# Reading the unsplit W_out blocks in one run: natural column order in a fused attention and MoE kernel

## The chip, the cores and the metric

The kernel runs on one core of one Trainium2 chip. The metric is the device time of one execution in microseconds. Three runs of the kernel before gave 651.16, 652.11 and 652.94 us; their median, 652.11 us, is the time before. The traced execution took 651.43 us, of which 649.9 us lie between its first and its last instruction.

## The reference

Attention with 4 sink tokens and a window of 128 over q, k, v of shape (4, 8, 768, 64), then a two-layer feed-forward block on the 3072 tokens that come out:

```
scores = (q @ k^T) / sqrt(64), masked to sinks and window
a      = exp(scores - max);  a = a / (sum + 1e-9)
x      = (a @ v)  as 3072 x 512
h      = x @ w_in                              (512 x 2048)
g      = max(h, 0) + alpha * min(h, 0)
out    = g @ w_out                             (2048 x 512)
```

The weights arrive as 64-bit floats and are turned into 32-bit ones on the chip.

## The kernel before

The tokens are cut into 12 chunks of 256 (`NCHUNK`), the hidden width of 2048 into 16 blocks of 128 (`NF`). For each chunk c the attention of 8 heads gives `xh` and `xl`, the two halves of x. For each block f, `gemm1(c, f)` multiplies x with block f of w_in into a PSUM bank, ScalarE and VectorE make g from it (L995, L996), and `gemm2(c, f)` adds g times block f of w_out (128 x 512) to the two output banks of the chunk, one for each half j of the tokens.

Most products are split: each factor is written as a high part of the type fp32r plus the rest, and three fp32r products (high x high, high x low, low x high) stand for the 32-bit one. In `gemm2` these are L1048, L1049 and L1046, three matmuls of 512 columns for each j. The split costs a cast on ScalarE and a subtraction on VectorE for g (L1001, L1002) and for the weights. In the first two chunks the first 8 blocks (`WHOLE = 8`, `c < 2 and f < WHOLE`) skip it: g and W_out stay whole, and `whole()` (L1035 to L1037) runs one native fp32 matmul for each j. A native fp32 matmul stands in the trace as two matmul instructions, so 2 chunks x 8 blocks x 2 halves give 64 of them at L1037.

The whole block lives in `entire` (128 x 512, written by `out_whole`, L449 to L452). When chunk 2 begins, `divide(f)` (L471 to L480) splits it: a cast to fp32r (L476, on ScalarE or VectorE) and a subtraction on VectorE (L479), 8 of each. From then on the block is read like the others, by `row` (L401, L402).

The order of columns: the host swaps the 512 columns of each W_out block (L1403) so that all even columns stand ahead of all odd ones. A matmul reads them through `rearrange("p (y x) -> p x y", y=2)`, which steps to and fro between the two halves of the row, 256 elements (1 KB) apart, and so meets the columns in their natural order. This alternating order is used for the split blocks and, before the change, for the whole ones at L1037 as well. `gemm1` reads x in the same way.

The order of instructions on each engine is written out by a planner. `Plan.draw` is a list scheduler: each operation has an engine and a cost in microseconds that the author gave it (for `whole()`, `2 * native(DM)`, which is 1.707), and at each step it takes the operation that can start first, with ties by rank. Each engine then runs its instructions in the planned order and waits on semaphores for what isn't ready. During chunks 0 and 1 the weights are loaded and converted as well: for each f < 8 ScalarE's L423 and VectorE's L427, L428, L440 (twice) and L453; for the other blocks L432, L435, L456, L462 and L465. The attention of chunk 1 is computed early in chunk 0's blocks, that of chunk 2 late in chunk 1's (`LATE = 11`).

Of the kernel before, what the change touches and what calls it, by code (L numbers as in the profile page):

```python
# [9 lines left out]
F32 = mybir.dt.float32  # L10
# [7 lines left out]
ALU = mybir.AluOpType  # L18

P = 128  # L20
B, H, S, D = 4, 8, 768, 64
DM, DF = 512, 2048
# [6 lines left out]
NF = DF // P  # L29
# [28 lines left out]
WHOLE = 8  # L58
# [28 lines left out]
class Plan:  # L87
# [20 lines left out]
    def held(self, tile_):  # L108
        v = Value(None)
        v.at = tile_  # L110
        return v
# [197 lines left out]
def dve(n, fast=False):  # L309
    return 0.07 + (0.52e-3 if fast else 1.04e-3) * n  # L310


def cast(n, psum=False):
    return (0.045 if psum else 0.092) + 0.84e-3 * n
# [22 lines left out]
def woven(n):  # L337
    return 0.003 + 0.4167e-3 * n


def native(n):
    return 1.667e-3 * n
# [3 lines left out]
ISSUE = 0.45  # L346
SINKLAG = 0.0
R_TAIL, N_TAIL, T_TAIL = 0.2, 0.65, 0.36


def program(ctx, tc, qk, pairs, vp, vq, vs, w, par, out):
    nc = tc.nc
# [5 lines left out]
    op, val, held = plan.op, plan.value, plan.held  # L358
# [36 lines left out]
    raws, fins = {}, {}  # L395
# [7 lines left out]


    def home(f):
        return f + NF - WHOLE if f < WHOLE else f

    def load_weights(f, engine="ACT"):
        raw = raws[f] = held(None)

        def run():
            raw.at = const.tile([P, 2 * DM, 2], I32, tag=f"w{home(f)}", name="wraw")
            (nc.sync if engine == "SP" else nc.scalar).dma_start(
                raw.at.rearrange("p (i x) w -> p i (x w)", i=2), w[f].bitcast(I32).rearrange("i p x -> p i x"))
        return op(engine, ISSUE if engine == "SP" else 0.12, run, writes=[raw] + (lent.get(home(f), []) if f < WHOLE else [raws[f - NF + WHOLE]]), nbytes=8 * P * 2 * DM)

    def convert_weights(f):
        raw, fin, wa = raws[f], Block(None), val("wa")
# [51 lines left out]

    def divide(f):  # L471
        fin, entire = fins[f], entires[f]

        def high(engine):
            fin.at[1] = const.tile([P, 2, DM], F32R, tag=f"out{f - 1}", name="wout")
            (nc.scalar.copy if engine == "ACT" else nc.vector.tensor_copy)(fin.at[1][:, 0], entire.at)  # L476
        op("ACT", cast(DM), lambda: high("ACT"), reads=[entire], writes=[(fin, 2)] + ([entires[f - 1]] if f else []),
           other=("DVE", dve(DM, True), lambda: high("DVE")))
        op("DVE", dve(DM), lambda: nc.vector.tensor_tensor(  # L479
            fin.at[1][:, 1], entire.at, fin.at[1][:, 0].bitcast(F32), ALU.subtract), reads=[entire, (fin, 2)], writes=[(fin, 3)])  # L480

    stage, vtile, vst = {}, {}, {}

    lent = {}
# [64 lines left out]
    part, alt = param[:, :4], param[:, 4:].bitcast(F32)  # L549
# [313 lines left out]
    turned = {}  # L863
# [143 lines left out]
    def gemm2(c, f, dst):  # L1007
        gh, gl = gs.pop((c, f))
        fin = fins[f]
        begin, end = (WHOLE % NF, (WHOLE - 1) % NF) if c == 2 else (0, NF - 1)  # L1010
        if f == begin:
            acc[c] = [val("pa"), val("s")] if c == 1 else [val("o"), val("o")]
        o2 = acc[c]
        if c == NCHUNK - 1 and f >= NF - 2:
            latest.append((f, fin, gh, gl))
            for j in range(2 if f == NF - 1 else 0):
                for x, fin, gh, gl in latest:
                    def last(j=j, x=x, fin=fin, gh=gh, gl=gl):
                        js = slice(j * P, (j + 1) * P)
                        nc.tensor.matmul(o2[j].at, gh.at[:, js], fin.row(0), start=False, stop=False)  # L1020
                        nc.tensor.matmul(o2[j].at, gh.at[:, js], fin.row(1), start=False, stop=False)
                        nc.tensor.matmul(o2[j].at, gl.at[:, js], fin.row(0), start=False, stop=x == NF - 1)
                    op("PE", 3 * woven(DM), last, reads=[fin, gh, gl], writes=[o2[j]], tail=R_TAIL)
                ob = val("ob")
                for n, cols in enumerate((slice(0, DM // 2), slice(DM // 2, DM)) if j else (slice(0, DM),)):
                    op("ACT", cast(cols.stop - cols.start, True), lambda ob=ob, j=j, cols=cols: nc.scalar.copy(ob.at[:, cols], o2[j].at[:, cols]),  # L1026
                       reads=[o2[j]], writes=[(ob, n)])
                    by, cost, engine = ("ACT", 0.1, nc.scalar) if n == j else ("SP", ISSUE, nc.sync)
                    op(by, cost, lambda ob=ob, j=j, cols=cols, engine=engine: engine.dma_start(dst(j)[:, :, cols], ob.at[:, cols]),
                       reads=[(ob, n)], nbytes=4 * P * (cols.stop - cols.start))  # L1030
            return
        if c < 2 and f < WHOLE:
            entire = entires[f]

            def whole():  # L1035
                for j in range(2):
                    nc.tensor.matmul(o2[j].at, gh.at[:, j * P:(j + 1) * P], entire.at.rearrange("p (y x) -> p x y", y=2),  # L1037
                                     start=f == begin, stop=False)
            op("PE", 2 * native(DM), whole, reads=[entire, gh], writes=o2, tail=N_TAIL)
            return  # L1040
        for lowpart in range(2):
            def some(lowpart=lowpart):
                for j in range(2):
                    js = slice(j * P, (j + 1) * P)
                    if lowpart:
                        nc.tensor.matmul(o2[j].at, gl.at[:, js], fin.row(0), start=False, stop=(f == end))  # L1046
                    else:
                        nc.tensor.matmul(o2[j].at, gh.at[:, js], fin.row(0), start=(f == begin), stop=False)  # L1048
                        nc.tensor.matmul(o2[j].at, gh.at[:, js], fin.row(1), start=False, stop=False)  # L1049
            op("PE", (2 if lowpart else 4) * woven(DM), some, reads=[fin, gl if lowpart else gh], writes=o2, tail=R_TAIL)  # L1050
        if f == end:
            for j in range(2):
                ob = val("ob")
                op("ACT", cast(DM, True), lambda ob=ob, j=j: nc.scalar.copy(ob.at, o2[j].at), reads=[o2[j]], writes=[ob],
           other=("DVE", dve(DM), lambda ob=ob, j=j: nc.vector.tensor_copy(ob.at, o2[j].at)) if 0 < c < 3 else None)
                op("SP", ISSUE, lambda ob=ob, j=j: nc.sync.dma_start(dst(j), ob.at), reads=[ob], nbytes=4 * P * DM)
            del acc[c]
# [109 lines left out]
    def dst(c):  # L1167
        return lambda j: out[c * QC:(c + 1) * QC].rearrange("(y j x) d -> j x y d", y=2, j=2)[j]
# [9 lines left out]
    n = 0  # L1178
# [35 lines left out]
    for a in pend:  # L1214
        gemm2(*a, dst(a[0]))
# [27 lines left out]
    gen = ctx.enter_context(tc.tile_pool(name="general", bufs=1))  # L1243
# [3 lines left out]
    wts = [fins[f].at for f in range(NF)]  # L1247
    with tc.If(bad != 0, label="general"):
        for f in range(NF):
            for i in range(2):  # L1250
                general_weights(nc, gen, w[f, i], wts[f][i])
        with tc.For_i(0, B, 1) as b:
            for cc in range(CPB):
                x = general(nc, gen, ptile, cc, b, qk5, vp5, nsink, window, ident)
                acc = [ptile("o", 2) for _ in range(2)]
                for f in range(NF):
                    general_moe(nc, gen, ptile, f, x, wts[f], alt, acc)
                for j in range(2):
                    ob = gen.tile([P, DM], F32, tag="ob", name="ob", bufs=3)
                    nc.scalar.copy(ob, acc[j])  # L1260
                    nc.gpsimd.dma_start(out5[b, cc, j], ob)
# [24 lines left out]
        nc.tensor.matmul(acc[j], gl[:, js], rows[0], start=False, stop=(f == NF - 1))  # L1286


def general_weights(nc, gen, src, dst):
    raw = gen.tile([P, DM, 2], I32, tag="wraw", name="wraw", bufs=2)  # L1290
    nc.gpsimd.dma_start(raw.rearrange("p x w -> p (x w)"), src.bitcast(I32))
    a = gen.tile([P, DM], I32, tag="wa", name="wa", bufs=2)
    low, high, af = raw[:, :, 0], raw[:, :, 1], a.bitcast(F32)
    nc.scalar.activation(af, high.bitcast(F32), AF.Abs)
    nc.vector.tensor_scalar(af, af, EXP_LOW, EXP_HIGH, op0=ALU.max, op1=ALU.min)
    nc.vector.tensor_scalar(a, a, 3, 0x3FFFFFFF, op0=ALU.logical_shift_left, op1=ALU.bitwise_and)
    nc.vector.scalar_tensor_tensor(a, high, -0x40000000, a, op0=ALU.bitwise_and, op1=ALU.bitwise_or)
    nc.scalar.activation(low, low.bitcast(U32), AF.Copy, scale=2.0 ** -29)
    nc.vector.tensor_tensor(a, a, low, ALU.add)
    nc.scalar.copy(dst[:, 0], af)  # L1300
    nc.vector.tensor_tensor(dst[:, 1], af, dst[:, 0].bitcast(F32), ALU.subtract)


def general(nc, gen, ptile, cc, b, qk5, vp5, nsink, window, ident):
# [118 lines left out]
```

## Time and profile before

| what | value |
|---|---|
| median of three runs | 652.11 us (651.16 to 652.94) |
| traced execution | 651.43 us, span 649.9 us |
| TensorE (PE) busy | 640.4 us, 99% of the span |
| VectorE (DVE) busy | 522.6 us, 80% |
| ScalarE (ACT) busy | 392.4 us, 60% |
| L1037, the native fp32 matmuls | 64, from 34.7 to 109.7 us, 36.5 us of busy time |

"Busy" for PE counts a modelled end of each matmul, and matmuls overlap: the duration of a matmul in the trace (705 ns at L1037) is not what it adds. What it adds is the distance from its start to the start of the next one. A first matmul after a slower one can show its start early, while it still queues behind it; the start after that one is then the reliable mark. PEld is the load of the stationary operand, which runs beside the matmul ahead of it.

### The profile page before, as it was taken

How to read it: one execution, taken by the hardware profiler on the slowest of the kernel's cores; microseconds unless marked ns; L12 is line 12 of the kernel's file. 1: busy time of each engine (PE TensorE's matmuls, PEld its weight loads, DVE VectorE, ACT ScalarE, POOL GpSimd, SP SyncE). 2: the span in 40 equal slices, each digit the busy share in tenths (PEclk: the TensorE clock that was granted, in tenths of full speed). 3: DMA queues.
4: the chain of work that ended last, by engine and by line, in shares of the span. 5: the costliest groups of instructions: out<-in, count | busy, mean ns of one | idle time of the engine just before them, and what ended most of it. 6: DMA issues, size and time to landing. Idle time of an engine off the chain costs nothing. (4 is left out here: it accounts for less than half of the span.)

```text
span 649.9 us, 13096 instructions
## 1 busy us (share of the span) xinstructions
PE 640.4 (99%) x4495; PEld 563.0 (87%) x4497; DVE 522.6 (80%) x1748; ACT 392.4 (60%) x1060; POOL 34.1 (5%) x115
## 2 busy tenths in 40 slices
PE   8999999989999999999999999999999999999997
PEld 3666667979998999999999999998999998998996
DVE  6998888997987987895996997895996997895332
ACT  6997677856646646645645754844754854752332
POOL 2120000000100000000100000000100000000000
PEclk9999999999999999999999999999999999999999
DMA  8776631333443444341633534432534424421001
GB/s 314 250 274 219 215 101 53 96 99 106 129 135 120 136 138 135 112 131 50 188 120 91 168 98 138 136 112 82 169 113 115 148 97 147 148 65 51 33 3 35
DMA packets 58825, 82.29 MB, mean 127 GB/s; under 512 B 9088, under 2 KB 35328, under 8 KB 58752
## 3 DMA queue, kind: packets, MB, share of 16 engines
q1 hardware_dynamic: 55200, 68.41, 33.3%
q10 hardware_dynamic: 3552, 12.98, 5.7%
q8 instruction: 37, 0.61, 0.4%
q14 instruction: 36, 0.29, 0.1%
HBM read 64.33 MB, written 17.04 MB: 125 GB/s over the span
## 5 line engine op out<-in xcount | busy, mean ns | idle before, releaser
L995 ACT ACTIVATE g<-bank,param 128x256 f32<-128x256 f32 x192 | 90.9, 473 | 94.4 <-PE bank L991 93.8
L991 PE MATMUL bank<-xh,win 128*128 128x256 f32 x768 | 140.5, 279 | 0.0
L991 PE MATMUL bank<-xh,w 128*128 128x256 f32 x768 | 139.1, 276 | 0.4 <-DVE g L996 0.4
L991 PEld LDWEIGHTS bank<-xh,w 128*128 128x128 f32 x768 | 120.9, 192 | 2.7 <-DVE g L996 1.0
L991 PEld LDWEIGHTS bank<-xh,win 128*128 128x128 f32 x768 | 120.8, 192 | 2.3 <-issue 1.6
L1001 ACT CAST gh<-g 128x256 fp32r<-128x256 f32 x176 | 70.6, 405 | 63.0 <-DVE g L996 62.4
L996 DVE TENSOR_TENSOR g<-bank,g 128x256 f32<-128x256 f32 x192 | 80.1, 420 | 33.8 <-ACT g L995 32.4
L991 PE MATMUL bank<-xl,win 128*128 128x256 f32 x384 | 105.7, 275 | 0.0
L991 PE MATMUL bank<-xl,w 128*128 128x256 f32 x384 | 105.6, 275 | 0.0
L700 ACT ACTIVATE pt<-pt,nm 128x260 f32<-128x260 f32 (+1 forms) x192 | 93.5, 489 | 16.5 <-DVE nm L694 16.2
L694 DVE CUSTOM_DVE_ANT_0 pt<-bank,masks 128x260 f32<-128x260 f32 (+1 forms) x192 | 71.2, 401 | 33.0 <-PE bank L680 29.3
L1002 DVE TENSOR_TENSOR gl<-g,gh 128x256 fp32r<-128x256 f32 x176 | 73.4, 421 | 17.6 <-ACT gh L1001 14.5
L991 PEld LDWEIGHTS bank<-xl,win 128*128 128x128 f32 x384 | 73.6, 192 | 2.3 <-issue 1.4
L991 PEld LDWEIGHTS bank<-xl,w 128*128 128x128 f32 x384 | 73.5, 192 | 1.2 <-issue 0.4
L1048 PE MATMUL bank<-w,gh 128*128 128x512 f32 x188 | 71.6, 381 | 0.0
L1049 PE MATMUL bank<-w,gh 128*128 128x512 f32 x188 | 71.2, 379 | 0.0
L641 ACT CAST kq<-stage 128x392 fp32r<-128x392 f32 (+1 forms) x80 | 39.1, 488 | 36.8 <-PE bank L680 28.2
L1048 PE MATMUL bank<-wout,gh 128*128 128x512 f32 x160 | 60.7, 379 | 0.0
L1049 PE MATMUL bank<-wout,gh 128*128 128x512 f32 x160 | 60.6, 379 | 0.0
L1046 PE MATMUL bank<-w,gl 128*128 128x512 f32 x188 | 56.4, 382 | 0.0
L1046 PE MATMUL bank<-wout,gl 128*128 128x512 f32 x160 | 47.7, 380 | 0.0
L745 POOL TENSOR_TENSOR sink<-pt,ri 128x8 f32<-128x8 f32 x80 | 20.2, 254 | 502.0 <-DVE ri L730 421.9
(150 smaller groups left out, 1106.3 us busy)
## 6 DMA issues: line engine op xcount, KB each, us to landing
stage<-qk SPq DMA_DIRECT2D x56, 324.0 KB, 2.9
wraw<-w ACTq DMA_DIRECT2D x12, 1024.0 KB, 5.2
swap<-comb SPq DMA_DIRECT2D x36, 256.0 KB, 2.0
comb<-swap SPq DMA_DIRECT2D x36, 256.0 KB, 3.0
stage<-qk SPq DMA_DIRECT2D x24, 260.0 KB, 2.7
out_dram<-ob SPq DMA_DIRECT2D x22, 256.0 KB, 2.7
v<-vq SPq DMA_DIRECT2D x24, 192.0 KB, 3.2
wraw<-w SPq DMA_DIRECT2D x4, 1024.0 KB, 9.2
```

The lines of the kernel that those rows point to most:

```text
L641: op("ACT", cast(KC - n), lambda: nc.scalar.copy(ks()[:, n:], k_raw()), reads=[st], writes=[(kq, "k")])
L694: o = op("DVE", dve(n), lambda: nc.vector.tensor_tensor_reduce(out=pt.at[:, u, w0], in0=s.at[:, w0], in1=masks[:, i, w0], scale=-0.125, sc ...
L700: op("ACT", exp(n), lambda: nc.scalar.activation(pt.at[:, u, w0], pt.at[:, u, w0], AF.Exp, bias=nm.at[:, h, u:u + 1], scale=-1.0, accum_ou ...
L745: op("POOL", 0.2, lambda: nc.gpsimd.tensor_tensor(sk.at[:, :, h], pt.at[:, :, P:P + NS], ri.at[:, :2].unsqueeze(2).broadcast_to([P, 2, NS] ...
L991: nc.tensor.matmul(h(), fin.win(part, ks), row, start=(kt == 0 and n == 0), stop=(kt == KT - 1 and n == 2))
L995: op("ACT", act(QC, True), lambda: nc.scalar.activation(g.at, h(), AF.Copy, scale=alt[:, f:f + 1]), reads=[bk, known("param")], writes=[g])
L996: op("DVE", dve(QC), lambda: nc.vector.tensor_tensor(g.at, h(), g.at, ALU.max), reads=[bk], writes=[g])
L1001: op("ACT", cast(QC), lambda: nc.scalar.copy(gh.at, g.at), reads=[g], writes=[gh])
L1002: op("DVE", dve(QC), lambda: nc.vector.tensor_tensor(gl.at, g.at, gh.at.bitcast(F32), ALU.subtract), reads=[g, gh], writes=[gl])
L1046: nc.tensor.matmul(o2[j].at, gl.at[:, js], fin.row(0), start=False, stop=(f == end))
L1048: nc.tensor.matmul(o2[j].at, gh.at[:, js], fin.row(0), start=(f == begin), stop=False)
L1049: nc.tensor.matmul(o2[j].at, gh.at[:, js], fin.row(1), start=False, stop=False)
```

## The change

The host leaves the columns of the first 8 W_out blocks in natural order and swaps only those of the other 8. `whole()` then reads `entire` in one run of 512 neighbouring elements. `divide` puts the columns into the alternating order: its cast and its subtraction read every second element of `entire` (steps of 8 bytes), twice 256, and write two runs of 256. The planned cost of `whole()` grows by 0.1 us, from 1.707 to 1.807. In `home` and `load_weights` an expression changes its form: with `NF = 16` and `WHOLE = 8`, `NF - WHOLE` and `NF // 2` are both 8, so every block gets the tile and the writes that it had. `general_weights` belongs to a branch that these inputs don't take.

```
     def home(f):
-        return f + NF - WHOLE if f < WHOLE else f
+        return f + NF // 2 if f < WHOLE else f
 ...
     def divide(f):
         fin, entire = fins[f], entires[f]
+        turned_ = lambda: entire.at.rearrange("p (x y) -> p y x", y=2)
+        part = lambda n: fin.at[1][:, n].rearrange("p (y x) -> p y x", y=2)
 ...
-            (nc.scalar.copy if engine == "ACT" else nc.vector.tensor_copy)(fin.at[1][:, 0], entire.at)
+            (nc.scalar.copy if engine == "ACT" else nc.vector.tensor_copy)(part(0), turned_())
 ...
-            fin.at[1][:, 1], entire.at, fin.at[1][:, 0].bitcast(F32), ALU.subtract), reads=[entire, (fin, 2)], writes=[(fin, 3)])
+            part(1), turned_(), part(0).bitcast(F32), ALU.subtract), reads=[entire, (fin, 2)], writes=[(fin, 3)])
 ...
             def whole():
                 for j in range(2):
-                    nc.tensor.matmul(o2[j].at, gh.at[:, j * P:(j + 1) * P], entire.at.rearrange("p (y x) -> p x y", y=2),
+                    nc.tensor.matmul(o2[j].at, gh.at[:, j * P:(j + 1) * P], entire.at,
                                      start=f == begin, stop=False)
-            op("PE", 2 * native(DM), whole, reads=[entire, gh], writes=o2, tail=N_TAIL)
+            op("PE", 2 * native(DM) + 0.1, whole, reads=[entire, gh], writes=o2, tail=N_TAIL)
 ...
-    w[:, 1] = inputs['moe_w_out'].reshape(NF, P, DM // 2, 2).swapaxes(2, 3).reshape(NF, P, DM)
+    w[:, 1] = inputs['moe_w_out'].reshape(NF, P, DM)
+    w[WHOLE:, 1] = inputs['moe_w_out'].reshape(NF, P, DM // 2, 2)[WHOLE:].swapaxes(2, 3).reshape(NF - WHOLE, P, DM)
```

## Rows read from the trace of the kernel before

**Rows 1.** Stages of the span: busy time (count) of each engine, clock, DMA.
```profile
34.60:51.00 16.40, 16.40 (x101) 10.16 (x100) 15.49 (x42) 14.57 (x37) 3.61 (x5) 1.00 0.67 228
51.00:66.00 15.00, 15.00 (x95) 10.21 (x94) 13.19 (x20) 11.06 (x21) 0.00 (x0) 1.00 0.64 227
66.00:98.00 32.00, 32.00 (x155) 20.46 (x154) 28.02 (x37) 23.76 (x36) 0.00 (x0) 1.00 0.49 167
98.00:110.40 12.40, 12.40 (x72) 9.27 (x71) 10.54 (x19) 9.99 (x17) 0.00 (x0) 1.00 0.13 51
110.40:150.00 39.60, 37.09 (x271) 33.03 (x271) 37.45 (x137) 25.95 (x73) 1.98 (x8) 1.00 0.28 85
250.00:600.00 350.00, 350.00 (x2578) 325.68 (x2576) 290.93 (x1050) 202.18 (x582) 16.33 (x57) 1.00 0.39 121
```

**Rows 2.** Line L1037: its matmuls, duration min/median/max in ns, first and last start.
```profile
L1037 PE MATMUL bank<-wout,g x64: 700/705/802, 34.7 to 109.7; 128*128 128x512 f32 x64
```

**Rows 3.** PE's instructions in order of time around 67 us: start, us, what.
```profile
67.01 0.28 PE L991 MATMUL bank<-xh,win 128*128 128x256 f32 x1
67.12 4.49 PE L1037 MATMUL bank<-wout,g 128*128 128x512 f32 x8
70.94 0.79 PE L991 MATMUL bank<-xh,win 128*128 128x256 f32 x1
71.56 0.28 PE L991 MATMUL bank<-xl,win 128*128 128x256 f32 x1
```

**Rows 4.** PE in order of time: fp32 operands read in one run.
```profile
33.74 0.71 PE L670 MATMUL bank<-stage 64*128 64x260 f32 x4
34.38 0.33 PE L719 MATMUL bank<-ident,pt 128*128 128x128 f32 x1
...
38.81 1.96 PE L873 MATMUL bank<-comb,v 128*64 128x256 f32 x24
40.70 0.71 PE L670 MATMUL bank<-stage 64*128 64x260 f32 x4
...
46.16 0.27 PE L719 MATMUL bank<-ident,pt 128*128 128x128 f32 x1
...
46.71 0.27 PE L720 MATMUL bank<-ident,pt 128*128 128x128 f32 x1
```

**Rows 5.** PE in order of time: fp32r, in one run (L680) and alternating (L1048).
```profile
113.18 0.29 PE L679 MATMUL bank<-kq 128*128 128x260 f32 x1
113.30 0.28 PE L680 MATMUL bank<-kq 128*128 128x260 f32 x1
113.43 0.38 PE L1048 MATMUL bank<-w,gh 128*128 128x512 f32 x1
113.64 0.38 PE L1049 MATMUL bank<-w,gh 128*128 128x512 f32 x1
```

**Rows 6.** L1037 alone in the first of these stages: PE busy (count), PEld busy (count).
```profile
34.60:51.00 16.40, 6.94 (x12) 1.99 (x12) 1.00 0.67 228
```

**Rows 7.** Groups by line and shape: count, busy us, mean ns, idle before.
```profile
L479 DVE TENSOR_TENSOR wout<-wout 128x512 fp32r<-128x512 f32 x8 | 5.5, 685 | 0.1
L476 ACT CAST wout<-wout 128x512 fp32r<-128x512 f32 x6 | 3.7, 620 | 3.1 <-DVE wout L479 3.1
L476 DVE CAST wout<-wout 128x512 fp32r<-128x512 f32 x2 | 0.8, 420 | 0.0
L440 DVE SCALAR_TENSOR_TENSOR wout<-wraw,wa 128x512 int32<-128x512 int32 x8 | 5.5, 691 | 0.0
```

**Rows 8.** Waits from 34.6 to 110.4 us: us, times, longest.
```profile
ACT g L995 <- PE bank L991: 10.6, 10, 2.4
```

**Rows 9.** Waits of PE from 110.4 to 150 us.
```profile
PE bank L815 <- DVE jk L741: 1.6, 2, 1.4
PE bank L991 <- DVE g L996: 0.4, 1, 0.4
```

More of the change, by code (lines that the diff above doesn't have):

```diff
@@ L414, in run @@
                 raw.at.rearrange("p (i x) w -> p i (x w)", i=2), w[f].bitcast(I32).rearrange("i p x -> p i x"))
-        return op(engine, ISSUE if engine == "SP" else 0.12, run, writes=[raw] + (lent.get(home(f), []) if f < WHOLE else [raws[f - NF + WHOLE]]), nbytes=8 * P * 2 * DM)
+        return op(engine, ISSUE if engine == "SP" else 0.12, run, writes=[raw] + ([raws[f - NF // 2]] if NF // 2 <= f < NF // 2 + WHOLE else lent.get(home(f), [])), nbytes=8 * P * 2 * DM)
     def convert_weights(f):
@@ L1250, in program @@
             for i in range(2):
-                general_weights(nc, gen, w[f, i], wts[f][i])
+                general_weights(nc, gen, w[f, i], wts[f][i], f < WHOLE and i == 1)
         with tc.For_i(0, B, 1) as b:
@@ L1286, in general_moe, with general_weights @@
         nc.tensor.matmul(acc[j], gl[:, js], rows[0], start=False, stop=(f == NF - 1))
-def general_weights(nc, gen, src, dst):
+def general_weights(nc, gen, src, dst, turned):
     raw = gen.tile([P, DM, 2], I32, tag="wraw", name="wraw", bufs=2)
@@ L1299, in general_weights @@
     nc.vector.tensor_tensor(a, a, low, ALU.add)
-    nc.scalar.copy(dst[:, 0], af)
-    nc.vector.tensor_tensor(dst[:, 1], af, dst[:, 0].bitcast(F32), ALU.subtract)
+    high, low = [dst[:, n].rearrange("p (y x) -> p y x", y=2) for n in range(2)]
+    af = af.rearrange("p (x y) -> p y x" if turned else "p (y x) -> p y x", y=2)
+    nc.scalar.copy(high, af)
+    nc.vector.tensor_tensor(low, af, high.bitcast(F32), ALU.subtract)
 def general(nc, gen, ptile, cc, b, qk5, vp5, nsink, window, ident):
```

## The prediction

> **What bounds the kernel now.** I read the stages first [rows 1]. From 250 us on, PE is busy all the time at a granted clock of 1.00 and VectorE (DVE) 290.93 of 350 us (83%): PE sets the pace, and the rest of the run begins as early as PE reaches it. Up to 110.4 us PE shows no idle time either. But other engines are close behind: DVE is busy 15.49 of 16.4 us (94.5%) from 34.6 to 51, with ScalarE at 14.57; then 51.75 of 59.4 us (87%) from 51 to 110.4; then 37.45 of 39.6 us (94.6%) from 110.4 to 150, and there PE does idle, 2.5 us. The reader is to see three stretches: PE and DVE nearly level, then PE ahead as the bound, then DVE as the bound.
>
> The next view is the line that changes. L1037 has 64 matmuls, from 34.7 to 109.7 us [rows 2]: all of them lie in the first two stretches. Its duration of 705 ns is a modelled one, so I take the spacing instead. Between the first matmul of a group of eight, at 67.12, and the first reliable start behind it, 71.56, lie the eight and one L991, which adds 0.11 (67.01 to 67.12): (4.44 - 0.11) / 8 = 0.541 us for each [rows 3]. All 64 are 34.6 us of PE.
>
> The last views are waits. From 34.6 to 110.4 us ScalarE's L995, the first step from `gemm1` to g, stands 10.6 us in 10 waits for PE [rows 8]: faster matmuls would be picked up. From 110.4 to 150 it is the other way round: PE waits 1.6 us for DVE's L741 and 0.4 for its L996 [rows 9]. L741 is chunk 2's softmax, which DVE must finish before the steady part begins.
>
> **The change, part by part.**
>
> *The moving operand of L1037 in one run.* Nothing is added or removed; each of 64 matmuls reads neighbours instead of stepping 1 KB to and fro. No row shows a native fp32 matmul of full width (128 columns of weights) with such a read, so I bound it. Six fp32 transposes of 128 columns, read in one run, begin 0.55 us apart from first to last, 0.11 each [rows 4]: for 512 columns, 0.44. The fp32 values of L873, two halves of the array's columns side by side, run 4 turns of 256 and 8 of 128 columns, 2048 in all, between 38.81 and 40.70, entry and exit included: 0.92 ns a column, 0.47 for 512 [rows 4]. The dear end is L670, fp32 in one run on two halves of the array's rows: two turns of 260 columns in 0.64 us, so 0.63 for 512 [rows 4]. Below the transposes I put the rate of one fp32r matmul twice, 2 x 0.215 = 0.43 [rows 5]. I take 0.44, from the transposes: like L1037 they use the whole array, with nothing beside them. So 64 x (0.541 - 0.44) = 6.5 us less PE time; the other values give 7.1 (0.43), 4.5 (0.47) and -5.7 (0.63, slower).
>
> The trace also holds a warning: for fp32r the alternating read is the cheaper one. L679 and L680 read 260 columns in one run and take 0.12 us each; L1048 reads 512 alternating in 0.21 [rows 5]. Scaled to 512 that is 0.24 against 0.21, 10% more for the single run. If fp32 followed fp32r, L1037 would go to 0.59 and the kernel lose 3.5 us. The Trainium skill speaks for the change here: "SBUF — State Buffer", under "Door 1: The DMA port swizzle", says that SBUF has lines of 16 bytes and that an access which moves to another line pays. By it every alternating read would be dear, and a run of four elements per line cheap. The fp32r rows don't agree with that, so I take the sum from the fp32 rows and not from the rule.
>
> *What of 6.5 us reaches the end.* In the first stretch are 12 of the 64 [rows 6], 1.2 us of the saving. DVE is busy 94.5% there, as in the stretch where it is the bound (94.6%) [rows 1]. So I count nothing for these 12. The other 52, 5.25 us, lie between 51 and 110.4 us, where DVE has 51.75 us of work in 59.4. If DVE can again be filled to 94.6%, it needs 54.7 us, so the stretch shrinks by 4.7 us at most. What DVE doesn't follow, PE loses later: the stretch after 110.4 is DVE's, and its PE waits grow by the same amount. With DVE filled to 92% it would be 3.2 us; with no idle left, all of the 5.25 and part of the 1.2. I take 4.7. What is late next is DVE's chain through chunk 2's softmax (L694, L741) up to about 150 us. Behind 150 us PE runs back to back, and nothing takes the gain back.
>
> *The split in `divide`.* Eight L479 on DVE (685 ns), six L476 on ScalarE (620) and two on DVE (420) now read every second element [rows 7]. Reads of that step cost DVE nothing in a two-input operation: L440 takes 691 ns for 512 elements of 8-byte step, against 685 for L479 [rows 7]. The two DVE casts run at twice that speed, and no row shows such a cast with a step; if they fell to L479's time it would be 2 x 0.27 = 0.5 us of DVE in the stretch where it counts. I take nothing, from L440's row, and keep 0.5 for the range. On ScalarE even 10% would be 0.4 us in all, beside its idle time (23.76 busy of 32 us [rows 1]); without that cover it would be those 0.4 us. The Trainium skill, "VectorE: DVE Perf Modes" under "Mode 2×_2P", asks of a one-source copy at double speed that both sides lie in SBUF and that the outermost dimension be even, not that the step be one; the pattern here is 2 x 256. By it the two casts stay at 420 ns; no row here shows it.
>
> *The planned cost.* The plan took 1.707 us for a pair of whole products; the trace has 4 x 0.541 = 2.16. Now it takes 1.807, against 4 x 0.44 = 1.76. A list scheduler may order differently from the first such pair on, on every engine, SP's and ScalarE's DMA issues too. No row gives that a price. I bound it by the waits that an order can make or spare in the DVE-bound stretch, some 2 us [rows 9], to either side, and take 0, because nothing in the rows points to one side.
>
> *The other edits* give the same tiles and writes (8 = 8), or lie in the branch not taken: 0.
>
> The sum: 651.43 - 4.7 = 646.7 us for the traced execution. It lies 0.7 us below the median of the runs, so I forecast 652.1 - 4.7 = 647.4.
>
> **The rivals.**
>
> *All of it arrives, or more.* DVE's idle time before 110 us follows from PE's lateness (10.6 us of ScalarE's waits [rows 8]), and an order planned at nearly the true cost may lose some of the 2 us of waits. For it: those waits; against it: DVE at 94.6% has not been filled further anywhere. 6.5 + 2 = 8.5 at most: 643.6 to 646, middle 645.3.
>
> *DVE takes it.* The conversions don't close up, and chunk 2's softmax starts almost where it did. For it: 94.6% and PE's wait for L741 [rows 1, 9]; against it: 7.65 us of DVE idle time between 51 and 110.4. A gain of 0.5 to 3 us: 649.1 to 651.6, middle 650.1.
>
> *The order of reading doesn't matter for native fp32.* Then L1037 stays at 0.541, the change doesn't do what it says, and 652.1 remains. For it: L670 reads in one run and needs 0.63 for 512, and fp32r gains nothing from it; against it: transposes and L873 [rows 4].
>
> *The single run is dearer.* PE, L1037, 64 times: at 0.59, as fp32r would have it, +3.5 us; at 0.63, as in L670, +5.7. It decides from 0.541 upward, and since PE has no idle time up to 110 us it all arrives: 655.6 to 657.8, middle 656.5. Against it the two cheaper rows of native fp32.
>
> *The new order is unlucky*: the 4.7 us and 2 more go into new waits in the DVE-bound stretch: 651 to 654.
>
> **How the numbers follow.** Forecast 0.50 (its own range 646.0 to 649.1); all or more 0.17; DVE takes it 0.15; order doesn't matter 0.08; dearer 0.04; unlucky order 0.06. A measurement of this kernel can tell about 0.3%, 2 us, from no change. Faster by over that: 0.50 + 0.17 + 0.09 of the 0.15 = 0.76. Slower: 0.04 + 0.03 of the 0.06 = 0.07. Within: 0.17. The range, 644.4 to 651.4, takes in most of the first three cases and leaves out about 2 in 10: the best of the second, and most of the last three.
>
> **What would show it.** Right: the spacing in an undisturbed group of eight at L1037 is 0.43 to 0.47; ScalarE's wait for PE before 110 us is shorter; DVE is fuller between 51 and 110; PE's waits for DVE from there to chunk 2's first `gemm1` are longer; and from then on the time between two chunks is the old one. Wrong: a spacing of 0.54 or more; or the spacing as forecast and a steady part that begins at the old time (DVE takes it) or over 6 us earlier; or DVE casts at L476 of 600 ns and more.

## The result, and the profile after

The changed kernel takes 642.91 us (median of 4 runs, 642.88 to 642.94), the kernel before in the same comparison 651.77 (651.16 to 652.94). The ratio is 0.986, with a 95% interval from 0.985 to 0.988: 8.9 us less. The forecast was 647.4, its range ended at 644.4. The direction was right, the size was not: nearly twice the 4.7 us arrived.

The same views as before. First the page of the kernel after: span, busy time of the engines, granted clock in 40 slices.

```profile
span 641.4 us, 13099 instructions
PE 633.8 (99%) x4495; PEld 564.1 (88%) x4497; DVE 522.5 (81%) x1748; ACT 392.7 (61%) x1060; POOL 33.8 (5%) x115
...
PEclk9999999999999999999999999999999999999999
```

L1037 is L1039 now. Its matmuls in the kernel after, and one group of eight in order of time, as in [rows 2, 3]:

```profile
L1039 PE MATMUL bank<-wout,g x64: 592/593/697, 34.8 to 102.9; 128*128 128x512 f32 x64
```

```profile
64.58 0.28 PE L993 MATMUL bank<-xh,win 128*128 128x256 f32 x1
64.69 3.60 PE L1039 MATMUL bank<-wout,g 128*128 128x512 f32 x8
67.72 0.67 PE L993 MATMUL bank<-xh,win 128*128 128x256 f32 x1
68.23 0.28 PE L993 MATMUL bank<-xl,win 128*128 128x256 f32 x1
```

From 64.69 to 68.23, less 0.11 for the L993 at 67.72, is 3.43 us for eight: 0.429 us each, where [rows 3] gave 0.541. Over 64 matmuls that is 7.2 us.

The stages of the kernel after, with the columns of [rows 1] (busy us and count of PE, PEld, DVE, ACT, POOL; clock; DMA share; GB/s). The last whole matmul starts at 102.9 us now, so the third stretch begins at 103.4 and not at 110.4:

```profile
34.60:51.00 16.40, 16.40 (x108) 11.25 (x109) 16.08 (x43) 15.47 (x41) 3.48 (x5) 1.00 0.64 229
51.00:66.00 15.00, 15.00 (x102) 11.06 (x101) 14.50 (x22) 12.62 (x23) 0.00 (x0) 1.00 0.61 230
66.00:98.00 32.00, 32.00 (x183) 24.44 (x182) 31.49 (x45) 27.54 (x40) 0.00 (x0) 1.00 0.51 186
98.00:103.40 5.40, 5.40 (x28) 3.49 (x27) 5.40 (x10) 4.10 (x9) 0.00 (x0) 1.00 0.00 0
103.40:142.00 38.60, 37.62 (x281) 33.88 (x279) 37.07 (x136) 26.44 (x73) 1.56 (x8) 1.00 0.28 87
250.00:600.00 350.00, 350.00 (x2573) 326.03 (x2572) 287.30 (x1034) 200.08 (x577) 15.88 (x56) 1.00 0.38 117
```

DVE, which I held to 94.6%, is busy 98.0% from 34.6 to 51 and 98.1% (51.39 of 52.4 us) from 51 to 103.4, and PE still shows no idle time there. The steady part (the last row) is as before.

PE's waits in the third stretch of the kernel after, which answer to [rows 9]:

```profile
PE bank L797 <- DVE ts L779: 0.8, 1, 0.8
PE bank L817 <- DVE wa L821: 0.2, 1, 0.2
```

I had forecast that PE's waits here would grow by what DVE could not follow. They shrank, from 2.3 us (the two lines of [rows 9], and a third of 0.3 us for L819 that those rows leave out) to 1.0. The comparison of the two orders shows why that may be: on PE, DVE and ScalarE the instructions after the first whole product are ordered differently, and the chain of chunk 2's softmax into its transposes is another one. So two things changed at once, and the experiments had to part them.

### The profile page after: what moved, and what is told of

Read it like the earlier page. It is cut to its first block, busy times and chain, and to the rows that moved or that the text cites. A ratio compares the mean times of both kernels' runs of the same rounds, so it can differ in the third digit from the quotient of the medians.

```text
span 641.4 us, 13099 instructions
## 1 busy us (share of the span) xinstructions
PE 633.8 (99%) x4495; PEld 564.1 (88%) x4497; DVE 522.5 (81%) x1748; ACT 392.7 (61%) x1060; POOL 33.8 (5%) x115
## 5 line engine op out<-in xcount | busy, mean ns | idle before, releaser
L997 ACT ACTIVATE g<-bank,param 128x256 f32<-128x256 f32 x192 | 90.4, 472 | 87.1 <-PE bank L993 86.5
L993 PE MATMUL bank<-xh,win 128*128 128x256 f32 x768 | 140.0, 279 | 0.0
L993 PE MATMUL bank<-xh,w 128*128 128x256 f32 x768 | 138.9, 276 | 0.0
L993 PEld LDWEIGHTS bank<-xh,w 128*128 128x128 f32 x768 | 121.1, 192 | 1.9 <-issue 0.7
L993 PEld LDWEIGHTS bank<-xh,win 128*128 128x128 f32 x768 | 120.9, 192 | 1.8 <-issue 1.1
L993 PE MATMUL bank<-xl,win 128*128 128x256 f32 x384 | 105.8, 276 | 0.0
L993 PE MATMUL bank<-xl,w 128*128 128x256 f32 x384 | 105.7, 275 | 0.0
L998 DVE TENSOR_TENSOR g<-bank,g 128x256 f32<-128x256 f32 x192 | 80.0, 420 | 31.4 <-ACT g L997 30.0
L993 PEld LDWEIGHTS bank<-xl,win 128*128 128x128 f32 x384 | 73.7, 192 | 1.7 <-issue 1.2
L993 PEld LDWEIGHTS bank<-xl,w 128*128 128x128 f32 x384 | 73.6, 192 | 1.1 <-issue 0.2
L1048 PE MATMUL bank<-w,gl 128*128 128x512 f32 x188 | 56.4, 382 | 0.0
L1048 PE MATMUL bank<-wout,gl 128*128 128x512 f32 x160 | 47.7, 380 | 0.0
```

The source lines that it names most:

```text
L993: nc.tensor.matmul(h(), fin.win(part, ks), row, start=(kt == 0 and n == 0), stop=(kt == KT - 1 and n == 2))
L997: op("ACT", act(QC, True), lambda: nc.scalar.activation(g.at, h(), AF.Copy, scale=alt[:, f:f + 1]), reads=[bk, known("param")], writes=[g])
L998: op("DVE", dve(QC), lambda: nc.vector.tensor_tensor(g.at, h(), g.at, ALU.max), reads=[bk], writes=[g])
```

## The experiments

Theory A: the faster matmuls save 7.2 us, all of which arrives, and the remaining 1.7 us come from the new order. Rival B: the order gives nothing, and faster matmuls spare waits by themselves. Rival C: DVE's cap (no more than 94.6% busy) holds as forecast, and the order gives the rest. The first four runs tell them apart. The kernel before took 652.66 us in that comparison (17 runs).

**The read alone** (label read_alone), with the order of before:

```
-                    nc.tensor.matmul(o2[j].at, gh.at[:, j * P:(j + 1) * P], entire.at.rearrange("p (y x) -> p x y", y=2),
+                    nc.tensor.matmul(o2[j].at, gh.at[:, j * P:(j + 1) * P], entire.at,
```

> The kernel before, with only the read at L1037 in one run; planned cost and so the order on every engine are those of before, and divide is untouched (the blocks keep the alternating order in memory, so the products of chunks 0 and 1 get their columns permuted: the output is left permuted there). Theory A (the matmuls' 64 x 0.112 = 7.2 us arrive whole, the other 1.7 of the 8.9 us come from the new order): 644.6 us. Rival B (order gives nothing, the faster matmuls by themselves also spare waits): 642.9. Rival C (VectorE's cap of the forecast holds and the order gives the rest): 647.1. All: spacing at L1037 0.43.

Measured: 645.55 us, ratio 0.990 (0.989 to 0.992), span 643.4 against 649.9: 6.5 us by the spans, 7.1 by the medians. A, not B and not C. From the first L1037 to the last it is 68.17 us in place of 75.07, 6.9 less; the first starts at 35.05 and not at 34.65, ahead of any changed instruction, which takes 0.4 of it in this execution. The last starts at 103.22 in place of 109.72. The stretch behind it has moved as a block: chunk 2's first value product (L873) comes 31.4 us later, as before (109.72 to 141.21 is 31.5), and PE waits there as it did. The wait is the same to the hundredth: in the kernel before it stood at 137.95 with 1.43 us; here, PE in order of time around it (the bracket is the idle time ahead):

```profile
128.77 0.60 PE L815 MATMUL bank<-ident,comb 128*128 128x128 f32 x4
129.13 0.36 PE L679 MATMUL bank<-kq 128*128 128x260 f32 x1
129.33 0.28 PE L680 MATMUL bank<-kq 128*128 128x260 f32 x1
129.45 0.49 PE L815 MATMUL bank<-ident,comb 128*128 128x128 f32 x3
131.37 0.33 PE L815 MATMUL bank<-ident,comb 128*128 128x128 f32 x1 [1.43 <-DVE jk L741]
131.91 0.60 PE L815 MATMUL bank<-ident,comb 128*128 128x128 f32 x2 [0.21 <-DVE jk L741]
```

Had DVE come later than PE into this stretch, the first of these waits would be longer. And DVE's rows of this kernel show that it could indeed be filled beyond 94.6%, with the old order: 98.0% up to 51 us and 96% (50.62 of 52.6 us) from there to 103.6:

```profile
34.60:51.00 16.40, 16.40 (x111) 11.32 (x108) 16.08 (x42) 15.13 (x39) 3.83 (x5) 1.00 0.69 235
51.00:66.00 15.00, 15.00 (x101) 11.06 (x101) 14.52 (x22) 13.06 (x24) 0.00 (x0) 1.00 0.65 233
66.00:98.00 32.00, 32.00 (x182) 24.18 (x181) 30.53 (x45) 26.27 (x38) 0.00 (x0) 1.00 0.52 186
98.00:103.60 5.60, 5.60 (x31) 3.74 (x29) 5.57 (x9) 5.49 (x11) 0.00 (x0) 1.00 0.00 0
```

**The order alone** (order_alone):

```
-            op("PE", 2 * native(DM), whole, reads=[entire, gh], writes=o2, tail=N_TAIL)
+            op("PE", 2 * native(DM) + 0.1, whole, reads=[entire, gh], writes=o2, tail=N_TAIL)
```

> The kernel before with only the planned cost of whole() raised by 0.1, so that its order is that of the changed kernel and the read stays alternating. A: 651.8 - 1.7 = 650.1 us. B: 651.8. C: 651.8 - 4.2 = 647.6. Spacing at L1037 stays 0.541.

Measured: 649.36 us, ratio 0.996 (0.994 to 0.997), span 647.9: 2.0 us by the spans, 3.3 by the medians. The spacing at L1037 is the old one: its duration is (700/705/802 ns), and the group of eight at 67.20 gives 0.541 us again (71.64 is the reliable start behind it). PE in order of time around chunk 2's softmax:

```profile
135.80 1.04 PE L815 MATMUL bank<-ident,comb 128*128 128x128 f32 x8
137.65 0.44 PE L795 MATMUL bank<-ident,ts 128*128 128x128 f32 x2 [0.81 <-DVE ts L777]
138.25 0.44 PE L815 MATMUL bank<-ident,comb 128*128 128x128 f32 x2 [0.16 <-DVE wa L819]
138.54 0.50 PE L894 MATMUL bank<-sinkT,vs 128*128 128x256 f32 x2
```

The 1.43 us are gone, 0.81 stand in their place. The spans add up: 6.5 for the read, 2.0 for the order, 8.5 for both (649.9 to 641.4). The medians don't add up (7.1 and 3.3, but 8.9 for both), because most executions of the kernel before have a mean granted clock of 0.994 to 0.997 and are longer for it, while those of order_alone have 0.999 or 1.000. Five of its 17 have 1.000, and four of them took 651.38 to 651.80 us (one 653.54); against these four order_alone's median is 2.0 to 2.4 us less, and read_alone's one execution at 1.000, 644.95, is 6.4 to 6.9 less. A holds; B falls, and so does C.

**The change with the old planned cost** (old_cost), which is the changed kernel without the order's part:

```
-            op("PE", 2 * native(DM) + 0.1, whole, reads=[entire, gh], writes=o2, tail=N_TAIL)
+            op("PE", 2 * native(DM), whole, reads=[entire, gh], writes=o2, tail=N_TAIL)
```

> The changed kernel with the planned cost of before (1.707 for a pair), so the order of before with the read in one run and the divide with its step of 8 bytes. A: 644.6 us, as read_alone. B: 642.9. C: 647.1. If the divide's step costs something where VectorE is the bound, this one lies up to 0.5 us above read_alone; if not, they agree.

Measured: 644.55 us (644.35 to 645.94), ratio 0.988 (0.987 to 0.990). As A has it. It lies 1 us below read_alone by the medians, and 0.4 to 0.6 by the executions at a granted clock of 1.000 (644.35 to 644.58, against the one of 644.95). It isn't longer, so no cost of the divide's new step can be seen in the time. It can be seen in its rows. The groups by line of old_cost and then of read_alone, which has the old divide (count, busy us, mean ns, idle before):

```profile
L481 DVE TENSOR_TENSOR wout<-wout 128x512 fp32r<-128x512 f32 x8 | 6.0, 752 | 0.2 <-ACT wout L478 0.2
L478 ACT CAST wout<-wout 128x512 fp32r<-128x512 f32 x6 | 4.2, 696 | 3.2 <-DVE wout L481 3.2
L478 DVE CAST wout<-wout 128x512 fp32r<-128x512 f32 x2 | 1.1, 540 | 0.0
```

```profile
L479 DVE TENSOR_TENSOR wout<-wout 128x512 fp32r<-128x512 f32 x8 | 5.5, 686 | 0.1
L476 ACT CAST wout<-wout 128x512 fp32r<-128x512 f32 x6 | 3.7, 621 | 3.1 <-DVE wout L479 3.1
L476 DVE CAST wout<-wout 128x512 fp32r<-128x512 f32 x2 | 0.8, 418 | 0.0
```

The new pattern costs 0.12 us on each DVE cast, 0.07 on each subtraction and on each ScalarE cast: 0.8 us of DVE in all. In the other kernels with this divide the means are 465 to 520 ns for the DVE casts and 739 to 792 for the subtractions, so the size varies with the order.

**The first three blocks alone** (first_three). This tests the step of the forecast that counted nothing for the 12 matmuls before 51 us:

```
-                    nc.tensor.matmul(o2[j].at, gh.at[:, j * P:(j + 1) * P], entire.at.rearrange("p (y x) -> p x y", y=2),
+                    nc.tensor.matmul(o2[j].at, gh.at[:, j * P:(j + 1) * P], entire.at if c == 0 and f < 3 else entire.at.rearrange("p (y x) -> p x y", y=2),
```

> The kernel before, the read in one run only for chunk 0 and blocks 0 to 2, which are the 12 of 64 matmuls between 34.6 and 51 us (columns permuted there). The forecast's step (VectorE at 94.5% leaves nothing to take there): 651.8 us, no change. Theory A or B (VectorE can be filled further, or isn't what PE waits for): 12 x 0.112 = 1.3 us less, 650.4.

Measured: 651.33 us, ratio 0.998 (0.997 to 0.999). Faster, though the interval only says by 0.5 to 2.0 us. The trace is sharper: from the first L1037 (35.52) to the last (109.35) it is 73.83 us, where it was 75.07; the first starts 0.87 later in this execution, ahead of any changed instruction. At the other end, the four executions at a granted clock of 1.000 took 650.11 to 650.44 us, against the 651.38 to 651.80 above. The 12 x 0.112 = 1.3 us arrive almost whole.

**What the read pays for.** Two kernels read with other patterns at L1037 and are the kernel before otherwise; one execution each, so I go by the spacing (the kernel before 652.39 us).

Runs of four (lines_of_four):

```
-                    nc.tensor.matmul(o2[j].at, gh.at[:, j * P:(j + 1) * P], entire.at.rearrange("p (y x) -> p x y", y=2),
+                    nc.tensor.matmul(o2[j].at, gh.at[:, j * P:(j + 1) * P], entire.at.rearrange("p (y x w) -> p x y w", y=2, w=4),
```

> The kernel before; L1037 reads runs of 4 elements (16 bytes) from the two halves of the row in turn, not single ones (columns permuted in chunks 0 and 1). If what the alternating read pays for is each move to another 16-byte line, a fourth of the moves: spacing between 0.43 and 0.46, near that of one run. If any pattern of two halves costs the same: 0.54.

Every second element (step_of_two):

```
-                    nc.tensor.matmul(o2[j].at, gh.at[:, j * P:(j + 1) * P], entire.at.rearrange("p (y x) -> p x y", y=2),
+                    nc.tensor.matmul(o2[j].at, gh.at[:, j * P:(j + 1) * P], entire.at.rearrange("p (x y) -> p y x", y=2),
```

> The kernel before; L1037 reads every second element, first the even, then the odd ones (8-byte steps, two elements in each 16-byte line; columns permuted in chunks 0 and 1). By lines of 16 bytes: 0.43 to 0.46. If any read with a step other than one element is dear: 0.54.

PE in order of time around a group of eight, of lines_of_four and then of step_of_two:

```profile
64.48 3.60 PE L1037 MATMUL bank<-wout,g 128*128 128x512 f32 x8
67.52 0.67 PE L991 MATMUL bank<-xh,win 128*128 128x256 f32 x1
68.03 0.28 PE L991 MATMUL bank<-xl,win 128*128 128x256 f32 x1
```

```profile
65.32 3.77 PE L1037 MATMUL bank<-wout,g 128*128 128x512 f32 x8
68.50 0.69 PE L991 MATMUL bank<-xh,win 128*128 128x256 f32 x1
69.03 0.28 PE L991 MATMUL bank<-xl,win 128*128 128x256 f32 x1
```

Less 0.11 and by eight: 0.430 and 0.450 us, against 0.429 in one run and 0.541 alternating. Stepping to and fro over 1 KB costs nothing when four neighbours are taken at a time; a step of two costs 0.02; single elements from two places in turn cost 0.11. So native fp32 pays for moves away from a group of neighbours. The Trainium skill ("SBUF — State Buffer", "Door 1: The DMA port swizzle") has 16-byte lines, four fp32, with at least two hits wanted in each for the full rate, and native fp32 nearly agrees with it: four hits 0.430, two 0.450, one 0.541.

The split blocks in one run (split_in_one_run), the same question for fp32r:

```
         def row(self, part):
-            return self.at[1][:, part].rearrange("p (y x) -> p x y", y=2)
+            return self.at[1][:, part]
```

> The kernel before; the split W_out blocks (L1046, L1048, L1049, L1020 to L1022) are read in one run and L1037 stays alternating (columns permuted). From L679 and L680 a run costs fp32r 10% more: spacing 0.236 for 512 columns, not 0.215, over some 1056 matmuls 22 us more: about 674 us. If fp32r is like fp32, no slower than before: 652 or less.

Measured, in one execution: 666.86 us, 14.5 more than before. PE in order of time in this kernel's steady part:

```profile
299.85 0.40 PE L1048 MATMUL bank<-w,gh 128*128 128x512 f32 x1
300.09 0.39 PE L1049 MATMUL bank<-w,gh 128*128 128x512 f32 x1
300.32 0.39 PE L1048 MATMUL bank<-w,gh 128*128 128x512 f32 x1
300.55 0.40 PE L1049 MATMUL bank<-w,gh 128*128 128x512 f32 x1
```

0.23 apart, where the alternating read gives 0.215 [rows 5]; 0.015 for each of the 1056 matmuls is 15.8 us, close to the 14.5. The warning in the forecast was right for fp32r, at 7% and not 10%: the two types want opposite orders, and for fp32r one element from each of two places is the cheaper read, against the rule just named. Why it is so stays open.

**Is the new order better for a reason?** Two other planned costs, with the read in one run (the kernel before 652.77 us).

```
-            op("PE", 2 * native(DM) + 0.1, whole, reads=[entire, gh], writes=o2, tail=N_TAIL)
+            op("PE", 2 * native(DM) + 0.01, whole, reads=[entire, gh], writes=o2, tail=N_TAIL)
```

> The changed kernel with the planned cost of whole() at 1.717, which is what the trace of after shows for a pair (4 x 0.429 us), not 1.807. Theory L (which order comes out is luck: any small change of a cost gives another order, better or worse by 2 us, and a truer cost isn't better): no better than 642.9, anywhere from 642.5 to 645. Rival T (a truer cost gives the better order): 642.9 or less, and the wait ahead of chunk 2's last transposes under 1.1 us.

The other has 0.2 in place of the 0.01 (cost_too_high).

> The changed kernel with a planned cost of 1.907 for whole(), 0.19 more than the pair takes. L: again 642.5 to 645, with no relation to the error. T: worse than the changed kernel, 643.5 to 645.

Measured: 644.87 us (644.33 to 645.58) with the true cost, 646.15 (645.77 to 647.99) with the one too high; the changed kernel, between them in cost, has 642.91. In both the wait for the softmax is back (1.6 us, and in cost_too_high another of 1.1). The truer cost gives no better order than the old one (old_cost 644.55), so T falls. The cost that is too high came out above both ranges, 645 at most, so L had the size wrong there. As far as these costs go, only 0.1 gives the good order, and nothing ties that to the true cost: it looks like luck, which four costs can't prove.

**Attention of chunk 2 earlier and later** (attention_earlier, attention_later):

```
-LATE = 11
+LATE = 12
```

> The changed kernel with the attention of chunk 2 spread over the last 12 steps of chunks 0 and 1 instead of 11 (LATE = 12). If VectorE's chain through chunk 2's softmax is what ends last ahead of the steady part, an earlier start spares up to the 1 us that PE still waits between 126 and 134: 641.9 to 642.5. If VectorE is full from 51 us on anyway, an earlier start only moves its work about: 642.9. Output as the reference.

The other has `LATE = 10`.

> The changed kernel with LATE = 10: the attention of chunk 2 begins one step later. If VectorE's chain ends last: the waits of PE ahead of the steady part grow by 1 to 2 us: 644 to 645. If not: 642.9.

Measured: 642.03 us (641.79 to 643.15) with 12, as forecast, and 645.44 with 10, a little more than forecast. PE's waits between 100 and 155 us, of attention_earlier and then of attention_later:

```profile
PE bank L993 <- DVE g L998: 0.4, 1, 0.4
```

```profile
PE bank L817 <- DVE jk L743: 1.7, 2, 1.5
PE bank L993 <- DVE g L998: 0.4, 1, 0.4
PE bank L817 <- DVE wa L821: 0.3, 1, 0.3
```

So the waits name the chain through chunk 2's softmax as what ends last ahead of the steady part; with the earlier start the wait for it is gone, with the later one it is back. But each value of LATE also gives a new order, and true_cost has the same wait with LATE at 11, so that the start by itself does it is not shown. LATE = 12 is 0.9 us below the changed kernel by the medians; the two were timed in different comparisons, with ratios of 0.984 (0.983 to 0.986) and 0.986 (0.985 to 0.988) to the kernel before, so that it beats the changed kernel is likely and not shown.

**Dummy matmuls in the old order's wait** (keep_warm). The profile of old_cost showed the granted clock at half for a while behind this wait, so I filled it, on top of old_cost:

```
-WARM = 60.0
+WARM = 160.0
```

> The run old_cost (the change with the order of before) with 9 short dummy matmuls put where the plan sees PE idle at L817, near 130 to 134 us, and nothing else. Theory (the old order's wait of 1.7 us and the ones beside it let the granted clock fall to half for 3.4 or 6.8 us in some executions, which costs 1.7 or 3.4 us then; the new order's shorter wait doesn't): the executions of this one agree within 0.3 us, as those of the changed kernel do, near old_cost's fastest, 644.4 us, and its profile shows no stretch below 1.00 between 100 and 600 us. Rival (the spread has another cause, such as the transfers at the start): it spreads over 1.5 us as before.

Measured: 644.55 us (644.35 to 645.07), and no stretch below 1.00 in its profile. The median is that of old_cost, whose one execution at a lower clock (0.996) took 645.94 us and the three at 1.000 644.35 to 644.58. All four executions with the dummies have 1.000 and still spread over 0.7 us, where I expected 0.3: that part of the spread is not the clock's. The last section has what the rows show.

## Why the prediction was wrong, point by point

- *The spacing.* Forecast 0.44, bounds 0.43 to 0.47 and 0.63 on the dear side; measured 0.429. The transposes were the right row [rows 4], L670 the wrong one. 6.5 us became 7.2: a term 0.7 us too small.
- *What of it reaches the end.* This step failed: "If DVE can again be filled to 94.6%, it needs 54.7 us, so the stretch shrinks by 4.7 us at most", and the nothing counted for the first 12. DVE was filled to 98% in the changed kernel, to 98 and 96% in the old order (read_alone), and the 12 gave 1.2 of 1.3 us (first_three). The busy share that DVE happens to have in one stretch is no limit in another. The prediction's argument that DVE "has not been filled further anywhere" was wrong of the trace before itself: the 94.6% came from where the stages were cut, and in the stretch from 33 to 50 us DVE was 97.6% busy (16.60 of 17 us) with no idle time of PE:

```profile
33.00:50.00 17.00, 17.00 (x111) 11.06 (x110) 16.60 (x43) 15.51 (x43) 4.36 (x6) 1.00 0.69 251
```

DVE's idle time from 34.6 to 110.4 us (8.6 us) was mostly (6.3 us) waiting for ScalarE, which waited for PE [rows 8], and it went when PE came sooner: up to 103.4 us it is 1.3 us in the kernel after. The two longest of DVE's waits before, then L997's wait for PE in the kernel after, which was L995's 10.6:

```profile
DVE g L996 <- ACT g L995: 2.6, 6, 0.9
DVE wa L435 <- ACT wa L423: 1.2, 2, 0.9
```

```profile
ACT g L997 <- PE bank L993: 2.5, 6, 1.0
```

That L423 was late because it stands behind L995 in ScalarE's order is read from this and not tested by itself. 0 + 4.7 should have been 1.2 + 5.3, or by the true spacing some 6.9 of 7.2. The prediction had named the sign: a steady part that begins over 6 us earlier.

- *The stretch behind.* I expected its waits to grow by what DVE could not follow. DVE followed, so the stretch moved as a block (read_alone), and the new order shortened it by 2.0 us (order_alone).
- *The order.* Priced at 0 with 2 us to either side: it gave 2.0, so the bound was right and the sign of it could not be known; the other costs give no reason for it.
- *Divide.* Counted at 0, kept 0.5 for the range; 0.8 us of DVE measured, not visible in the time. L440 was the wrong row to go by: the subtraction went from 686 to 752 ns. The casts neither kept 420 ns, as the conditions cited in the prediction would have it, nor fell to 685: 516 in the changed kernel, 540 in old_cost.
- *The range.* The rival in which all arrives, or more, named both parts (up to 8.5 us, 643.6) at a chance of 0.17; the result, 642.91, lay 0.7 us past its end, as much as the spacing was mis-sized by. Its two halves were independent of each other, and I let the weaker argument, the cap, carry half of the chance.

## What to carry to other kernels

Where one engine shows no idle time and another is "nearly full", look at what the nearly full one waits for: if its gaps end with the first engine's results, they are slack that can close, as here, and its busy share is no cap. A change of a planner's cost is a change of the whole order: time it by itself, since here it gave a quarter of the gain, and two costs close by did not. Read native fp32 operands in runs of four neighbours or more (a step of two cost little here); don't carry that over to fp32r without a row of its own.

## What the runs showed of the hardware that was not expected

Reading order has opposite effects on the two 32-bit types: per 512 columns native fp32 takes 0.429 us in one run and 0.541 alternating, fp32r 0.23 and 0.215.

A wait of PE of 1.4 us, with shorter ones behind it, can be followed by a stretch in which the granted clock is at its lower level, 1.2 GHz. The stages of first_three at that place, where PE waited 1.43 us for L741 at 137.60 and twice 0.2 soon after (the columns are those of [rows 1]):

```profile
134.00:142.00 8.00, 6.04 (x30) 4.48 (x30) 7.49 (x32) 3.10 (x10) 0.36 (x2) 0.80 0.01 3
142.00:150.00 8.00, 8.00 (x55) 6.65 (x54) 6.07 (x15) 2.89 (x6) 0.00 (x0) 0.78 0.36 101
```

The means of 0.80 and 0.78 are made of 1.0 and 0.5: taken by single microseconds, the clock is 0.50 from 139 to 145. In this execution the kernel took 653.30 us, 3.2 more than its fastest of 650.11. Of the ten kernels profiled here with that wait (1.4 to 1.6 us), six show such a stretch behind it and four, the kernel before among them, don't; of the four without it (the changed kernel, order_alone, attention_earlier and keep_warm, which fills it) none does. That fits the scatter: the executions of the changed kernel lie within 0.06 us of each other and those of order_alone within 0.22, while the 17 of the kernel before lie within 2.3. The mean granted clock of each execution bears it out: of first_three's twelve, the four at 1.000 took 650.11 to 650.44 us, the three at 0.996 or 0.997 650.91 to 651.36, the five at 0.994 652.26 to 653.30; the kernel before goes the same way but for its 653.54 at 1.000. It isn't the cause of all scatter: attention_earlier, at 0.999 to 1.000, spreads over 1.4 us. Nor is it shown why the same wait is followed by the lower level in some executions only.
